# A third place for Q's and K's halves in the head of an attention-plus-MLP kernel, with two buffers of rows to be turned in place of three

## The chip, the core and the metric

The kernel runs on one core of a Trainium2 chip. TensorE (PE) multiplies matrices into PSUM, ScalarE (ACT) and VectorE (DVE) work on tiles, GpSimd (POOL) does small things, and DMAs are issued from the queues of SyncE (SP), POOL and ACT. Each engine works through its own instructions in the order of the program; engines wait for one another by semaphores. The metric is the device time of one execution in microseconds. The time before is the median of three runs.

## What is computed

```python
x  = A_x                                   # 1 x 2048 x 640
xn = layernorm(x)
q, k, v = split(xn @ wqkv, 32 heads of 20)
p  = softmax(q @ k.T * 20 ** -0.5)         # per head, 2048 x 2048
a  = (p @ v) @ wo
y  = layernorm(xn)
m  = gelu(y @ w1 + b1) @ w2 + b2           # 640 -> 1536 -> 640
return x + a + m
```

## The kernel before

All matrix products of the projections and the MLP are made from pairs of 16-bit halves: a value is written as a high half and a low half in float16 (the low half is what the high half's rounding left), and a product is three matmuls (high by high, high by low, low by high; `PASS`, line 326).

The work has two stages. In the **head** (lines 175 to 665) x is normalised, turned so that features lie on partitions, and projected to Q, K and V, while the weights of the MLP are loaded, squared for their scale and split into halves. In the **main part** (from line 668) attention and MLP are woven together by hand on TensorE. Both stages have `tc.manual_schedule()`: what stands in the program first goes first on its engine, and nothing is reordered.

The head goes over four blocks of 512 tokens, `for c in range(4)` (line 585). For each block:

- `qk(c, tt)` for `tt` = 0 to 4 (lines 328 to 341, called at 593 and 598): 30 matmuls fill one PSUM tile with 256 features of Q or K for the 512 tokens.
- Then some slices of the weights' work, `some(n)` (line 534), or a step of the next block's norm: `norm_a`, `norm_b`, `norm_c` (lines 245 to 286). `norm_c` writes the reciprocal deviations to `rscr` in DRAM by a DMA that POOL issues (line 286).
- Then `qk_out(c, tt, ps)` (line 346): ScalarE writes the high half of the PSUM tile to `qkhl` (line 352), VectorE the low half (353), the squares of the high half are taken (`qk_sq`, 363), and two DMAs on SP's queue bring both halves to `qkscr` in DRAM (358). The tile `qkhl` is of the pool `st`, tag `ks`, which has two buffers; a buffer is free again once its two DMAs have landed and its squares are taken. Later the same two buffers take the attention's K tiles.
- In the blocks c = 1 and c = 2, behind the outputs tt = 2, 3 and 4, `turn(nxt, j)` (line 312, called at 627 to 629) prepares the next block: j = 0 behind tt = 2, j = 1 and 2 behind tt = 3, j = 3 behind tt = 4. ScalarE writes the high half of 128 tokens' rows to `row` (318), VectorE the low half (319), and a transposing DMA on SP's queue turns it into the block's tile `xnt` (320). A buffer of `row` is free again when its transpose has landed. Behind j = 3 the whole turned block is written to `xscr` (323). Block 1 is turned on TensorE instead (`transp`).
- Then four `vproj(c, j)` (line 404): 30 matmuls each, for V of 128 tokens, with their output `vproj_out` (416).

All these PSUM tiles, and the small ones for scales (`mxp`, line 112), go round in the three buffers of tag `s` of the pool `psS`: a matmul that takes a buffer waits until the tile of three allocations before has been read. `pow2` (line 104) sums a tile of squares over partitions by a matmul with ones (line 114); `factors()` (456) does so for the bias `b1t`, whose square ScalarE takes through `squares` (97). In block c = 1 `factors()` and the first slice of w2's split (139 to 141) are the slices called at tt = 4, between the product `qk(1, 4)` and its output.

`junk` is a scratch that receives the elementwise results of square activations whose only wanted output is the sum (`accum_out`). `sums("k", ...)` and `sums("v", ...)` (lines 605 and 611) take the squares of K's and V's weights.

After `load_x(3)` on SP's queue (line 633) block 3's rows come to the tiles `xt`; `norm_a(3)` reads them at c = 2, tt = 0.

Of the kernel before, what the change touches and what calls it, by code (L numbers as in the profile page):

```python
# [10 lines left out]
F16 = mybir.dt.float16  # L11
BF16 = mybir.dt.bfloat16
# [6 lines left out]
P = 128  # L19
S, D, H, DH, F = 2048, 640, 32, 20, 1536  # L20
KD = D // P
# [23 lines left out]
def mha_mlp_kernel(tc, x, wqkv, wo, w1, b1, w2, b2, out):  # L45
# [4 lines left out]
    with (  # L50
# [40 lines left out]
        def squares(ws, junk):  # L91

            acc = sm.tile([P, 8], F32, tag="acc", name="acc")
            for i, w in enumerate(ws):
                j = junk[:, : w.free_size()] if len(w.shape) == 2 else (
                    junk[:, : w.shape[1] * w.shape[2]].rearrange("p (a b) -> p a b", a=w.shape[1]))
                nc.scalar.activation(j, w, AF.Square, accum_out=acc[:, i : i + 1])
            return acc[:, : len(ws)]
# [76 lines left out]
        with tc.tile_pool(name="pa", bufs=2) as pa, tc.tile_pool(name="pa1", bufs=1) as pa1, tc.manual_schedule():  # L175
            wv = pa1.tile([P, KD, 3, 2, D], F16, name="wv")

            stage = {}
# [96 lines left out]
            def norm_b2(c):  # L275
                mv, ve, r, r2 = rs[c]

                nc.vector.tensor_mul(ve, r, r)
                nc.vector.scalar_tensor_tensor(ve, ve, 2.0**-20, mv[:, :, 1], ALU.mult, ALU.mult)
                nc.vector.tensor_scalar(ve, ve, EPS, None, ALU.add)  # L280
                nc.gpsimd.tensor_tensor(r2, ve, nhalf, ALU.pow)

            def norm_c(c):
                mv, ve, r, r2 = rs.pop(c)
                newton(r2, ve, "b")
                nc.gpsimd.dma_start(rscr[c * 512 : (c + 1) * 512].rearrange("(j p) -> p j", p=P), r2)
# [25 lines left out]
            def turn(c, j):  # L312

                if j == 0:
                    xnts[c] = pa.tile([P, KD, 2, 512], F16, tag="xnt", name=f"xnt{c}")
                xv = xts[c][j].rearrange("p (k n) -> p k n", k=KD)
                row = pa.tile([P, KD, 2, P], F16, tag="row", name="row", bufs=3)
                nc.scalar.activation(row[:, :, 0, :], xv, AF.Copy)
                nc.vector.tensor_sub(row[:, :, 1, :], xv, row[:, :, 0, :])
                nc.sync.dma_start(xnts[c].rearrange("p k s t -> p (k s) t")[:, :, j * P : (j + 1) * P],  # L320
                                  row.rearrange("p k s n -> p (k s n)"), transpose=True)
                if j == 3:
                    nc.sync.dma_start(xscr[:, :, :, c * 512 : (c + 1) * 512], xnts[c])
                    del xts[c]
# [16 lines left out]
                return ps  # L341

            norms = [None, None]
            pend = []

            def qk_out(c, tt, ps):
                hl = stp.tile([P, 2, 2, 512], F16, tag="ks", name="qkhl")

                parts = ((0, 2),) if tt != 2 else ((0, 1), (1, 2))
                for i0, i1 in parts:  # L350
                    a = qks[:, (2 * tt + i0) // KD : (2 * tt + i0) // KD + 1]
                    nc.scalar.activation(hl[:, 0, i0:i1], ps[:, i0:i1], AF.Copy, scale=a)  # L352
                    nc.vector.scalar_tensor_tensor(hl[:, 1, i0:i1], ps[:, i0:i1], a, hl[:, 0, i0:i1],  # L353
                                                   ALU.mult, ALU.subtract)
                if c + tt > 0:
                    qk_sq(c, tt, hl)
                for s in range(2):
                    nc.sync.dma_start(
                        qkscr[s, 2 * tt * P : (2 * tt + 2) * P, c * 512 : (c + 1) * 512]
                        .rearrange("(i p) t -> p i t", p=P), hl[:, s])  # L360
                return hl

            def qk_sq(c, tt, hl):
                if tt % 2:
                    sq = stp.tile([P, S // 2], F16, tag="qs", name="sq").bitcast(BF16).rearrange("p (i t) -> p i t", i=2)
                else:
                    sq = pa.tile([P, 2, 512], BF16, tag="sq", name="sq", bufs=2)
                if c == 0:
                    nc.scalar.activation(sq, hl[:, 0], AF.Square)
                else:  # L370
                    nc.vector.tensor_mul(sq, hl[:, 0], hl[:, 0])
                pend.extend((c, 2 * tt + i, sq[:, i]) for i in range(2))
# [50 lines left out]
                                                   ALU.mult, ALU.subtract)  # L423

            qks = pa1.tile([P, 2], F32, name="qks")
            junk = pa1.tile([P, 3 * D], BF16, name="junk")
            accs = {}

            def sums(tag, ws):
                accs[tag] = squares(ws, junk)  # L430
# [97 lines left out]
            def ask(n):  # L528
                for _ in range(n):
                    next(asked, None)  # L530
# [3 lines left out]
            def some(n):  # L534
                for _ in range(n):
                    next(slices, None)
# [48 lines left out]
            for c in range(4):  # L585
                nxt = c + 1 if c < 3 else None
                for tt in range(5):
                    if c == 0 and tt == 1:
                        norm_b2(0)
                        norm_c(0)  # L590

                        nc.scalar.activation(junk[:, :1], ones[:, :1], AF.Exp)
                        ps = qk(0, 1, lambda: scale_of("k"))
                        hl = qk_out(0, 0, first)
                        split_qkv("q", c0=4 * P)
                        split_qkv("k")
                    else:
                        ps = qk(c, tt)
                    if tt == 3:
                        lengths(4)  # L600

                    if c == 0:
                        if tt == 0:
                            split_qkv("q", c0=2 * P, c1=4 * P)
                            sums("k", [stage["k"][:, 0:3], stage["k"][:, 3:]])
                            first = ps
                            continue
                        elif tt == 1:
                            qk_sq(0, 0, hl)
                        elif tt == 2:  # L610
                            sums("v", [stage["v"][:, 0:3], stage["v"][:, 3:]])
                            norm_a(1)
                        elif tt == 3:
                            scale_of("v")
                            split_qkv("v")
                    else:

                        step = tt - (c == 1)
                        if nxt and 0 <= step < 3:
                            (norm_a, norm_b, norm_c)[step](nxt)  # L620
                            some(1)
                        else:
                            some(2)
                    qk_out(c, tt, ps)

                    ask((0, 1, 2, 2, 1)[tt] if c == 0 else 0)
                    if nxt and c > 0 and tt >= 2:
                        for j in ((0,), (1, 2), (3,))[tt - 2]:
                            turn(nxt, j)
                    if c == 3 and tt == 2:  # L630
                        early = [load_features(mc) for mc in range(2)]
                if c == 1:
                    load_x(3)
                if c == 3:
                    stack = load_stack(0, 0)
                    for _ in range(6):
                        next(stack)
                for j in range(4):
                    ps = vproj(c, j)
                    if j == (0 if c == 3 else 1):  # L640
                        lengths(10)
                    if c + j > 0:

                        vproj_out(c, j, ps)
                    if c == 0:
                        if j < 2:
                            (norm_b, norm_c)[j](1)

                        pts = []
                        for k in ((), (0,), (2, 4), ())[j]:  # L650
                            transp(1, k, pts)
                        for t in pts:
                            transp_out(*t)
                    if j == 0 and c == 3:
                        shifts()
                        for _ in stack:
                            pass
                    some(1 if c == 3 else 2 if j < 3 or c == 0 else 0)
                    if c + j == 0:
                        vproj_out(c, j, ps)  # L660
                    if c == 0:
                        ask(2 if j == 0 else 1)
                if c == 0:
                    load_x(2)
# [678 lines left out]
```

## Time and profile before

| | us |
|---|---|
| runs: median of 3 | 1332.87 |
| lowest and highest run | 1332.36, 1333.18 |
| the profiled execution: its span | 1337.9 |
| its distance from the median of the runs | 5.0 |
| TensorE busy | 1325.8 |
| ScalarE busy | 1128.0 |
| VectorE busy | 1055.1 |

For the profiled execution its span is the only time there is: from the first instruction to the last. A row of the timeline gives an instruction's (or some merged instructions') start and duration, the engine, the line of the kernel, the operation, output and inputs, shapes and count; in brackets how long the engine was idle before it, and what ended the wait. A row of the waits gives who waited for whom, the microseconds in total, how often, and the longest. A row of the windows gives, for a stretch, its length, the busy time of each engine with the count of its instructions, the clock that TensorE was granted, the DMA engines' share and GB/s. In rows of the timeline a queue is written SPq, and PEld is TensorE's weight load.

### The profile page before, as it was taken

What the parts mean: (1) busy time and instruction counts of PE and PEld (TensorE: products, weight loads), DVE (VectorE), ACT (ScalarE), POOL (GpSimd) and SP (SyncE); (2) the same over time, 40 slices, a digit from 0 to 9 for tenths busy, and PEclk for the clock granted to TensorE, in tenths of its full rate; (3) what the DMA queues carried; (4) which work ended last, traced back from release to release, by engine and by line L of the source; (5) the groups of instructions that cost most, each with busy time, mean ns of one, the idle gap of its engine ahead of it and who ended that gap; (6) DMA issues with size and microseconds to landing.
All of it is one profiled execution on the core that took longest, in us unless ns stands there. A gap on an engine that the chain in (4) does not pass through costs nothing.

```text
span 1337.9 us, 29042 instructions
## 1 busy us (share of the span) xinstructions
PE 1325.8 (99%) x11635; PEld 586.7 (44%) x11635; DVE 1055.1 (79%) x1431; ACT 1128.0 (84%) x1306; POOL 37.5 (3%) x86
## 2 busy tenths in 40 slices
PE   9999899999999999999999999999999999999998
PEld 6645456444434343434343443344443434333366
DVE  7656754998788989878897879888879888997742
ACT  7844334999999999999999999999999999999900
POOL 3010000000000000000000000000000000000000
PEclk9999899999999999999999999999999999999999
DMA  9778723021203232212322132223032323334375
GB/s 279 254 196 176 136 79 104 15 59 39 66 28 103 61 83 81 63 48 59 111 63 81 33 93 66 75 69 94 19 80 71 93 66 87 118 95 118 105 218 188
DMA packets 100326, 129.54 MB, mean 97 GB/s; under 512 B 24292, under 2 KB 66664, under 8 KB 100188
## 3 DMA queue, kind: packets, MB, share of 16 engines
q1 hardware_dynamic: 96652, 120.25, 31.6%
q0 software_dynamic: 2912, 6.90, 2.8%
q8 instruction: 92, 1.51, 0.5%
q10 hardware_dynamic: 624, 0.51, 0.1%
q14 instruction: 46, 0.38, 0.1%
HBM read 82.14 MB, written 42.51 MB: 93 GB/s over the span
## 4 chain that ended last, share of the span: by engine, by line
PE 87%; DVE 6%; DMA 4%; ACT 1%; issue 1%; SPq 0%; ACTq 0%; DVEq 0%
PE o L779 30%; PE s L748 20%; PE py L1061 13%; PE pu L1031 11%; PE z L1146 5%; PE qkp L337 5%; PE vp L410 3%; DVE low L762 2%; DMA xt<-in_A_x_dram 1%; DMA xnt<-row 1%; DMA qkscr<-qkhl 1%; DVE st L255 1%; DVE qkhl L353 1%; ACT p L750 1%; DMA wos<-in_A_wo_dram 0%
## 5 line engine op out<-in xcount | busy, mean ns | idle before, releaser
L750 ACT ACTIVATE p<-s 128x1024 f32<-128x1024 f32 x1024 | 973.9, 1050 | 33.1 <-PE s L748 27.1
L762 DVE TENSOR_TENSOR low<-p 128x1024 f16<-128x1024 f32 x512 | 614.3, 1218 | 144.8 <-ACT p L750 144.0
L779 PE MATMUL o<-p,vfull 128*32 128x512 bf16 (+1 forms) x4096 | 429.0, 493 | 0.0
L748 PE MATMUL s<-qs,ks 61*128 61x512 f16 x2048 | 311.4, 381 | 0.2 <-ACT p L750 0.2
L748 PEld LDWEIGHTS <-ks 61*128 61x128 f16 x2048 | 61.2, 94 | 278.4 <-issue 276.1
L1061 PE MATMUL py<-w2t,hT 128*128 128x320 f16 x1152 | 178.5, 300 | 0.0
L1031 PE MATMUL pu<-xm,w1t 128*128 128x256 f16 x1440 | 178.2, 273 | 0.1
L1031 PEld LDWEIGHTS <-w1t 128*128 128x128 f16 x1440 | 131.0, 98 | 64.0 <-issue 50.2
L1061 PEld LDWEIGHTS <-hT 128*128 128x128 f16 x1152 | 102.3, 98 | 88.1 <-issue 53.9
L337 PE MATMUL qkp<-xnt,wv 128*128 128x512 f16 x600 | 131.1, 379 | 1.3 <-issue 1.3
L779 PEld LDWEIGHTS <-vfull 128*32 128x32 f16 x3072 | 59.9, 95 | 138.4 <-issue 106.9
L779 PE MATMUL o<-low,vfull 128*32 128x512 f16 x1024 | 101.3, 377 | 0.1
L337 PEld LDWEIGHTS <-wv 128*128 128x128 f16 x600 | 58.2, 98 | 71.0 <-issue 1.6
L779 PEld LDWEIGHTS o<-p,vfull 128*32 128x32 f32 x2048 | 61.7, 108 | 53.2
L410 PE MATMUL vp<-wv,xnt 128*128 128x320 f16 x480 | 69.5, 306 | 3.7 <-DVE qkhl L353 3.7
L1146 PE MATMUL z<-w1t,ot 128*128 128x320 f16 x480 | 67.4, 299 | 0.0
L352 ACT ACTIVATE qkhl<-qkp,qks 128x1024 f16<-128x1024 f32 (+1 forms) x24 | 23.1, 964 | 46.3 <-PE qkp L337 26.6
L410 PEld LDWEIGHTS <-xnt 128*128 128x128 f16 x480 | 47.9, 100 | 23.8 <-issue 3.7
L1146 PEld LDWEIGHTS <-ot 128*128 128x128 f16 x480 | 46.0, 98 | 22.9 <-issue 5.5
L353 DVE SCALAR_TENSOR_TENSOR qkhl<-qkp,qks,qkhl 128x1024 f16<-128x1024 f32 (+1 forms) x24 | 26.5, 1104 | 32.9 <-ACT qkhl L352 32.9
L1103 DVE SCALAR_TENSOR_TENSOR acc<-z,sc,acc 128x320 f32<-128x320 f32 x32 | 17.5, 549 | 37.3 <-PE z L1146 37.2
L800 ACT ACTIVATE ev<-o 128x512 f32<-128x512 f32 x64 | 39.5, 618 | 2.2 <-PE o L779 2.1
(195 smaller groups left out, 670.4 us busy)
## 6 DMA issues: line engine op xcount, KB each, us to landing
qkscr<-qkhl SPq DMA_DIRECT2D x40, 256.0 KB
opart<-ev SPq DMA_DIRECT2D x124, 80.0 KB
ks<-qkscr SPq DMA_DIRECT2D x120, 80.0 KB
qs<-qkscr SPq DMA_DIRECT2D x192, 40.0 KB
oa<-opart SPq DMA_DIRECT2D x32, 240.0 KB
xt<-in_A_x_dram SPq DMA_DIRECT2D x16, 320.0 KB
xscr<-xnt SPq DMA_DIRECT2D x4, 1280.0 KB
xm<-xscr SPq DMA_DIRECT2D x8, 640.0 KB
```

The costliest lines, as they stand in the source:

```text
L337: nc.tensor.matmul(ps[:, i, :], wv[:, k, q, a, mm * P : (mm + 1) * P], xnts[c][:, k, b, :], start=(k + n == 0), stop=(k == KD - 1 and n == 2))
L352: nc.scalar.activation(hl[:, 0, i0:i1], ps[:, i0:i1], AF.Copy, scale=a)
L353: nc.vector.scalar_tensor_tensor(hl[:, 1, i0:i1], ps[:, i0:i1], a, hl[:, 0, i0:i1], ALU.mult, ALU.subtract)
L410: nc.tensor.matmul(ps[:, hf, :320], xnts[c][:, k, a, j * P : (j + 1) * P], wv[:, k, 2, b, hf * 320 : (hf + 1) * 320], start=(n == 0), stop ...
L748: nc.tensor.matmul(ps[:, a, :], ks[64 * a : 64 * a + 61, kb * P : (kb + 1) * P], qs[64 * a : 64 * a + 61, cc * 512 : (cc + 1) * 512], star ...
L750: nc.scalar.activation(pt, ps, AF.Exp, scale=QS)
L762: nc.vector.tensor_sub(low, pt, upper(pt))
L779: nc.tensor.matmul(pv.o[32 * q : 32 * q + 32, :], src[:, v0 - PAD * (1 - q % 2) :][:, :32], t, start=q not in pv.begun, stop=last, skip_gr ...
L800: nc.scalar.activation(evs[g, hf][:, cc], pv.o, AF.Copy)
L1031: nc.tensor.matmul(ps[:, i], w1v[:, k, (f + i) // 4, a, fo_ : fo_ + P], xnt[:, k, b, :], start=(n == 0), stop=(n == 3 * KD - 1))
L1061: nc.tensor.matmul(ps[:, :320], hTs[mc][:, f, a, j * P : (j + 1) * P], w2v[:, f, b, hf * 320 : (hf + 1) * 320], start=(n == 0), stop=(n == ...
L1146: nc.tensor.matmul(ps[:, :320], ot[:, k, a, j * P : (j + 1) * P], wov[:, k, b, h * 320 : (h + 1) * 320], start=(n == 0), stop=(n == 3 * KD ...
```

## The change

Three edits, all in the head.

1. The tile of rows to be turned (`row`) has two buffers, the pool's default, in place of three.
2. `qk_out` counts its calls. Each third tile `qkhl` gets a place of its own (pool `pa1`, one buffer, tag `hl`); the others go round in the two buffers of tag `ks` as before. So there are three places in turn.
3. `junk` is 1536 elements long in place of 1920, and the squares of K's and V's weights (five slabs of 640) are taken in three pieces (2, 2 and 1 slabs) in place of two (3 and 2).

```diff
@@ turn
-                row = pa.tile([P, KD, 2, P], F16, tag="row", name="row", bufs=3)
+                row = pa.tile([P, KD, 2, P], F16, tag="row", name="row")
                 nc.scalar.activation(row[:, :, 0, :], xv, AF.Copy)
                 nc.vector.tensor_sub(row[:, :, 1, :], xv, row[:, :, 0, :])
@@ qk_out
             norms = [None, None]
+            outs = [0]
             pend = []
 
             def qk_out(c, tt, ps):
-                hl = stp.tile([P, 2, 2, 512], F16, tag="ks", name="qkhl")
+                outs[0] += 1
+                third = outs[0] % 3 == 0
+                hl = (pa1 if third else stp).tile([P, 2, 2, 512], F16, tag="hl" if third else "ks", name="qkhl")
@@ scratch
-            junk = pa1.tile([P, 3 * D], BF16, name="junk")
+            junk = pa1.tile([P, F], BF16, name="junk")
@@ the head's loop
-                            sums("k", [stage["k"][:, 0:3], stage["k"][:, 3:]])
+                            sums("k", [stage["k"][:, 0:2], stage["k"][:, 2:4], stage["k"][:, 4]])
...
-                            sums("v", [stage["v"][:, 0:3], stage["v"][:, 3:]])
+                            sums("v", [stage["v"][:, 0:2], stage["v"][:, 2:4], stage["v"][:, 4]])
```

## The prediction

> **What bounds the kernel now.** First the page: its span and its busy row.
>
> ```profile
> span 1337.9 us, 29042 instructions
> PE 1325.8 (99%) x11635; PEld 586.7 (44%) x11635; DVE 1055.1 (79%) x1431; ACT 1128.0 (84%) x1306; POOL 37.5 (3%) x86
> ```
>
> TensorE is busy for 1325.8 of 1337.9 us. All that the diff touches runs in the head, before the attention's first score matmul at 224.70 in the timeline. Second, TensorE's waits up to 226 us, and then ScalarE's (line waited for: us in total, times, longest).
>
> ```profile
> PE vp L410 <- DVE qkhl L353: 3.7, 1, 3.7
> PE qkp L337 <- issue: 1.3, 1, 1.3
> ...
> ACT row L318 <- DMA xnt<-row: 6.5, 1, 6.5
> ACT qkhl L352 <- DMA qkscr<-qkhl: 6.3, 1, 6.3
> ```
>
> TensorE loses only 3.7 + 1.3 us to waits in the whole head. ScalarE waits 6.3 us for a place of Q's and K's halves (qkhl), which a third place can take away, and 6.5 us for a buffer of rows (row), of which there will be one less. So I look for where these two waits sit. The timeline around the turning of block 2's rows (c = 1; start, duration, engine, line):
>
> ```profile
> 94.36 1.35 ACT L318 ACTIVATE row<-xt 128x640 f16<-128x640 f32 x2
> 94.47 1.49 SPq L320 DMA_TRANSPOSE xnt<-row  x1
> 94.74 0.79 POOL L286 DMA_DIRECT2D rscr<-r  x1 [3.21 <-DVE lo L117]
> 95.61 0.20 ACT L97 ACTIVATE junk<-b1t 128x12 bf16<-128x12 f32 x1
> 95.71 0.19 ACT L97 ACTIVATION_READ_ACCUMULATOR junk<-b1t 128x1 f32 x1
> 95.80 0.82 ACT L139 ACTIVATE wtmp<-w2t,s 128x640 f32<-128x640 f32 x1
> 100.24 0.28 PE L114 MATMUL mxp<-acc,ones 128*128 128x1 f32 x2
> 100.38 8.31 PE L410 MATMUL vp<-wv,xnt 128*128 128x320 f16 x60
> 100.49 1.11 ACT L352 ACTIVATE qkhl<-qkp,qks 128x1024 f16<-128x1024 f32 x1 [3.87 <-issue]
> 103.64 1.27 DVE L353 SCALAR_TENSOR_TENSOR qkhl<-qkp,qks,qkhl 128x1024 f16<-128x1024 f32 x1
> 108.14 0.74 ACT L318 ACTIVATE row<-xt 128x640 f16<-128x640 f32 x1 [6.54 <-DMA xnt<-row]
> 111.57 1.36 SPq L320 DMA_TRANSPOSE xnt<-row  x1
> 113.83 3.56 PE L410 MATMUL vp<-wv,xnt 128*128 128x320 f16 x25
> 118.66 26.06 PE L337 MATMUL qkp<-xnt,wv 128*128 128x512 f16 x120 [1.26 <-issue]
> 119.20 3.89 SPq L192 DMA_DIRECT2D xt<-in_A_x_dram  x4
> ```
>
> Rows 1 and 2 of the four (counted from 0) are written at 94.36 as a pair. Row 3 has to wait for row 0's buffer, that is for the landing of the transpose issued at 94.47, until 108.14. Nothing on TensorE needs that row soon, so the wait is free today but for the 1.26 us at 118.66, where Q and K of block 2 wait for the block's turned rows. The same stretch for block 3 (c = 2), and the clock around it:
>
> ```profile
> 125.88 0.88 DVE L255 BATCH_NORM_STATS2 st<-xt 128x6 f32<-128x320 f32 x2
> 140.19 0.77 POOL L286 DMA_DIRECT2D rscr<-r  x1 [2.00 <-DVE r L243]
> 144.72 1.38 SPq L320 DMA_TRANSPOSE xnt<-row  x1
> 144.99 6.65 PE L337 MATMUL qkp<-xnt,wv 128*128 128x512 f16 x30
> 151.63 1.11 ACT L352 ACTIVATE qkhl<-qkp,qks 128x1024 f16<-128x1024 f32 x1 [6.30 <-DMA qkscr<-qkhl]
> 152.64 1.35 ACT L318 ACTIVATE row<-xt 128x640 f16<-128x640 f32 x2
> 155.12 1.10 ACT L352 ACTIVATE qkhl<-qkp,qks 128x1024 f16<-128x1024 f32 x1
> 156.11 0.73 ACT L318 ACTIVATE row<-xt 128x640 f16<-128x640 f32 x1
> 158.17 1.28 DVE L353 SCALAR_TENSOR_TENSOR qkhl<-qkp,qks,qkhl 128x1024 f16<-128x1024 f32 x1
> 159.50 6.88 PE L410 MATMUL vp<-wv,xnt 128*128 128x320 f16 x30 [3.67 <-DVE qkhl L353]
> 159.96 0.82 DVE L319 TENSOR_TENSOR row<-xt,row 128x640 f16<-128x640 f32 x1
> ...
> 158.00:159.00 1.00, 0.00 (x0) 0.00 (x0) 1.00 (x2) 0.69 (x2) 0.00 (x0) 0.55 1.08 210
> 164.00:165.00 1.00, 1.00 (x5) 0.59 (x4) 0.73 (x2) 0.00 (x0) 0.00 (x0) 0.53 0.00 0
> ```
>
> The last two rows are of the windows view; the number after POOL's pair is the granted clock. Here the 6.30 us wait for a qkhl place makes the next output late: ScalarE at 155.12, VectorE at 158.17 to 159.45. That frees the PSUM place which the second block of V needs, and TensorE stands for 3.67 us. The clock falls to a half at about 158.1 and is back at about 164.9, so TensorE works 5.4 us, from 159.50 on, at half speed: another 2.7 us. This place costs 3.67 + 2.7 = 6.4 us, and it is what the third place can win back.
>
> **The change, part by part.**
>
> *Two buffers of rows.* Row 2 now takes row 0's buffer, so the wait moves from row 3 forward to row 2, in ScalarE's order from 108.14 up to the second of the pair at 94.36. That second one started at about 94.36 + 1.35 - 0.74 = 95.0. What stands behind it on ScalarE is no longer harmless: the square of b1t (95.61), its accumulator (to 95.90), a weight split (95.80), and the output of the last Q/K product (100.49). The b1t sum feeds the two small mxp matmuls, and these stand on TensorE at 100.24, ahead of all of V's product (100.38). TensorE works in order, so it will stand from 100.24 until row 2, b1t and the sum are done. With row 2 at 108.14, the sum is ready 95.90 - 95.0 = 0.9 us later, at 109.05, and V's product starts some 0.35 us after that, near 109.4 instead of 100.38: 9.0 us lost.
>
> Does the landing stay at 108.14? It isn't governed by how many transposes queue up, but by the 2 KB write of rscr in four-byte pieces, issued by POOL right behind the transpose:
>
> ```profile
> rscr<-r POOLq DMA_DIRECT2D x4, 2.0 KB, 11.6
> ```
>
> (page, DMA issues; the last number is the median to landing.) 94.74 + 11.6 = 106.3, and the transpose is seen 1.8 us later. Neither issue moves. Bounds: not before 106.3 if rscr holds it (1.8 us less), not after 108.14 + 1; I take 108.14. The Trainium skill ("DMA: Bandwidth & Descriptors", Queues, rings and completion order) says that a DMA's semaphore increment lands only after every earlier write of that DMA engine, across its queues. By that rule the landing cannot come before rscr's writes are through; the 108.14 agrees.
>
> The clock: a gap of 3.67 us was enough to halve it, so one of 9 us is. The nearest row says 2.7 us for the way back; with the 6.8 us of half clock used in full it would be 3.4, and with a restart late in them as little as 1.5. The Trainium skill ("TensorE: Matmul & The Clock Gate", The HAM clock gate) counts some 3.4 us at half speed after a restart, which would be 1.7 us; the trace has 5.4 us at half speed, and the measurement goes into the sum.
>
> The output behind (ScalarE near 110, VectorE near 113.8 instead of 103.64, done by 115.1) frees the PSUM place for V's second block, due at 109.4 + 4.1 + up to 2.7, about 116: just in time. V's four blocks took 100.38 to 117.39, so they end near 109.4 + 17.0 + 2.7 = 129.1. The last row's transpose is issued near 116.5 (VectorE's part stands behind the late output; 111.57 before), so it lands before 129 and the 1.26 us at 118.66 is gone. Q and K of block 3 start at 129.1 instead of 118.66: **+10.4 us**.
>
> *The third place.* The fourth output of c = 2 takes the place of the first, not the second, whose transfer was late; the 6.30 us wait goes. What is late next: row 2 again, now waiting for the transpose of 144.72. With 108.14 - 94.74 = 13.4 us after rscr's issue it lands at about 140.19 + 13.4 = 153.6 in the old frame (estimate; the row at 156.11, which had no wait, bounds it from above). With nothing else changed ScalarE would then reach the next output at about 155.4 instead of 155.12, VectorE, with one row's subtraction (0.82) already done, at 157.2 instead of 158.17, and TensorE would still stand 2.7 us.
>
> But VectorE has a lead now. Its long queue in c = 2 starts with the statistics at 125.88, when the x rows land (issued at 119.20 on SP, behind the last transpose). That transpose moves by 116.5 - 111.57 = 5 us, TensorE by 10.4. So VectorE's chain, up to the rscr write of 140.19, comes about 5 us earlier in TensorE's time, and so does the landing: 148.6. Row 2 then ends at 149.3 and the split behind it near 150.6, before the last Q/K product ends at 144.99 + 6.65 = 151.64. The output goes at 151.7, VectorE is through by 154.2, and V's second block, due at 155.8, doesn't wait. **-3.67 - 2.7 us.** Bounds for this part: -6.4 to -1.0.
>
> *Squares of K's and V's weights in three pieces, shorter scratch.* The same elements, one more activation and accumulator each:
>
> ```profile
> 20.84 1.79 ACT L97 ACTIVATE junk<-w2t 128x1920 bf16<-128x1920 f32 x1
> 22.75 1.27 ACT L97 ACTIVATE junk<-w2t 128x1280 bf16<-128x1280 f32 x1
> 25.15 0.28 PE L114 MATMUL mxp<-acc,ones 128*128 128x2 f32 x2
> 25.29 15.70 PE L337 MATMUL qkp<-xnt,wv 128*128 128x512 f16 x72
> ```
>
> A piece of 1920 takes 22.75 - 20.84 = 1.91 us with its accumulator, one of 1280 about 1.4, one of 640 about 0.86 (by the slope), so three take 3.65 against 3.3: 0.35 us more. K's sum, done near 24.1, is due at 25.15, so that is hidden; the K weights' split behind it feeds TensorE closely. Bounds 0 and 0.4 us; I take 0.2. For V's sum VectorE's statistics are the later wait: nothing.
>
> *The sum:* 9.0 + 2.7 - 1.3 - 3.7 - 2.7 + 0.2 = +4.2 us on the profile's span of 1337.9. The profiled execution is 5.0 us longer than the median of the runs (1332.87); I carry the difference over: **1337.1**. The rest of the program is fed by TensorE's own pace and only moves.
>
> **The rivals.**
>
> *The first transpose lands in time (faster).* If, with less in SP's queue, row 0's transpose landed before 100.24 - 0.9 = 99.3, row 2 would wait on nobody's account and only the 6.4 us would be won: about 1326.7. The time falls one for one with the landing; it decides at about 108.14 - 4.2 = 103.9. For it: the bare issue takes 1.49 us. Against it: rscr's 11.6 us. By the ordering rule quoted above it can't happen while rscr is issued there. 0.08; landings between some 103 and 106.5, no measurable difference, 0.14.
>
> *The second stall stays.* If VectorE has no lead, only 1.0 of the 6.4 us is won: +9.6, 1342.5. For it: x rows and wo's pieces arrive by DMA, not at TensorE's pace. Against it: only 1 to 2 us of the 5 are needed. 0.15. By the Trainium skill ("TensorE: Matmul & The Clock Gate", The HAM clock gate) the clock falls after an idle window of some 3.4 us, so that a stand of 2.7 us would cost no clock and this case would give 1339.8; the trace's clock fell 2.3 us into the idle time, so I don't count on it.
>
> *The freed wait is no place at all:* were the 6.30 us owed to SP's queue and not to the place, the third place would give nothing, and the result is that of the case before it. In its 0.15.
>
> **How the numbers follow.** The forecast, 1334.5 to 1339, has 0.58; slower for a cause I don't see (tiles of the attention lying on other old ones) 0.05. About 0.2% (2.7 us) is what a measurement of this kernel can tell from no change: 1330.2 and 1335.5 are the borders. Below the first: 0.08. Between: 0.14 and about 0.08 of the forecast's lower end, 0.22. Above: 0.70. The range, 1332 to 1342.5, leaves out the fast rival, the earliest landings and half of the slow case: under 0.2.
>
> **What would show it.** TensorE's largest wait in the head at its mxp matmul near 100, some 9 us, released by ScalarE's b1t; ScalarE's wait for the transpose of row 0 at the second row of the pair; the clock at a half behind it; no idle time before Q and K of block 3; no wait of ScalarE on qkscr<-qkhl, and none of V's product on L353. It is wrong if that ScalarE wait is under 9 us, or if V's product still stands in block 3.

## The result and the profile after

| | median, us | lowest to highest | runs |
|---|---|---|---|
| before | 1333.06 | 1332.36 to 1334.49 | 5 |
| changed | 1341.60 | 1341.00 to 1344.01 | 5 |

The ratio is 1.0066 (1.0054 to 1.0079): 8.5 us slower. The forecast was +4.2 us, 1337.1. The profiled execution of the changed kernel tells something else at first sight: its span is 1338.9 us, only 1.0 us over the 1337.9 of before. The same execution took 1341.0 us by the clock that the runs are timed with, so 2.1 us lie outside the span. By that difference the profile of before belongs to an execution of about 1340.0 us (an estimate), though the five runs shown of before end at 1334.5. That will be the point on which the sum failed.

The changed kernel, the waits of TensorE and of ScalarE up to 226 us (line waited for: us in total, times, longest; from line 346 on its lines are numbered three higher than before):

```profile
PE mxp L114 <- ACT junk L97: 6.5, 1, 6.5
PE warm L235 <- POOL ones L197: 1.1, 1, 1.1
...
ACT row L318 <- DMA xnt<-row: 18.0, 3, 10.9
```

Before, TensorE stood for 3.7 us ahead of V's second block of c = 2 and for 1.3 us ahead of the Q/K product of block 2; both waits are gone. In their place stands the b1t sum, for 6.5 us, behind ScalarE's square (L97). ScalarE now waits 18.0 us for transposes of rows, 6.5 before, and no longer for places of qkhl. The timeline of the changed kernel around the turning of block 2's rows:

```profile
94.16 1.49 SPq L320 DMA_TRANSPOSE xnt<-row  x1
94.43 0.79 POOL L286 DMA_DIRECT2D rscr<-r  x1 [3.18 <-DVE r L243]
94.80 0.73 ACT L318 ACTIVATE row<-xt 128x640 f16<-128x640 f32 x1
106.40 0.74 ACT L318 ACTIVATE row<-xt 128x640 f16<-128x640 f32 x1 [10.87 <-DMA xnt<-row]
107.04 0.20 ACT L97 ACTIVATE junk<-b1t 128x12 bf16<-128x12 f32 x1
107.38 0.58 PE L114 MATMUL mxp<-acc,ones 128*128 128x1 f32 x2 [6.48 <-ACT junk L97]
107.83 9.73 PE L413 MATMUL vp<-wv,xnt 128*128 128x320 f16 x60
```

Row 1 is written at 94.80, row 2 only at 106.40, when row 0's transpose, issued at 94.16, has landed. b1t's square, which before stood at 95.61, follows at 107.04, and TensorE takes the sum at 107.38. The 60 matmuls of V behind it take 9.73 us; before they took 8.31. The windows of the same kernel (after the pair of POOL: granted clock, DMA share, GB/s) show why V is slower:

```profile
104.00:106.00 2.00, 0.00 (x0) 0.00 (x0) 0.00 (x0) 0.00 (x0) 0.00 (x0) 0.50 1.33 76
108.00:110.00 2.00, 2.00 (x9) 1.14 (x8) 1.69 (x15) 1.05 (x2) 0.00 (x0) 0.50 1.15 237
110.00:112.00 2.00, 2.00 (x14) 1.31 (x13) 1.90 (x8) 0.00 (x0) 0.00 (x0) 0.81 1.16 88
```

All engines stand from 104 to 106, and the clock is at a half by then. A mean of 0.81 over 110 to 112 means half speed until about 110.8. In c = 2, where block 3's rows are turned, the changed kernel goes on without a stop:

```profile
145.81 0.77 POOL L286 DMA_DIRECT2D rscr<-r  x1 [2.00 <-DVE r L243]
150.34 1.38 SPq L320 DMA_TRANSPOSE xnt<-row  x1
152.20 1.11 ACT L355 ACTIVATE qkhl<-qkp,qks 128x1024 f16<-128x1024 f32 x1 [1.27 <-PE qkp L337]
158.05 0.74 ACT L318 ACTIVATE row<-xt 128x640 f16<-128x640 f32 x1 [4.11 <-DMA xnt<-row]
159.92 1.09 ACT L355 ACTIVATE qkhl<-qkp,qks 128x1024 f16<-128x1024 f32 x1
161.69 1.28 DVE L356 SCALAR_TENSOR_TENSOR qkhl<-qkp,qks,qkhl 128x1024 f16<-128x1024 f32 x1
163.13 4.24 PE L413 MATMUL vp<-wv,xnt 128*128 128x320 f16 x30
```

The fourth output of c = 2 goes at 152.20, as soon as its product is there; row 2 waits 4.11 us for its buffer, the next output follows at 159.92, VectorE is through at 162.97, and V's second block starts at 163.13 with no idle time: by a hair. The landing keeps its distance from the write of rscr, not from the transpose's own issue: row 2 is written 7.7 us after the transpose was issued (150.34) and 12.2 us after the write (145.81); in block 2 it was 12.2 and 12.0 us.

### The profile page after: what moved, and what is told of

It reads as the page before. It is cut to its first block, busy times and chain, and to the rows that moved or that the text cites. A ratio compares the mean times of both kernels' runs of the same rounds, so it can differ in the third digit from the quotient of the medians.

```text
span 1338.9 us, 29043 instructions
## 1 busy us (share of the span) xinstructions
PE 1325.0 (99%) x11635; PEld 586.4 (44%) x11635; DVE 1055.4 (79%) x1431; ACT 1129.5 (84%) x1310; POOL 37.5 (3%) x86
## 4 chain that ended last, share of the span: by engine, by line
PE 90%; DVE 5%; DMA 2%; ACT 1%; issue 1%; SPq 0%; DVEq 0%; ACTq 0%
PE o L782 29%; PE s L751 19%; PE py L1064 12%; PE pu L1034 11%; PE qkp L337 8%; PE vp L413 5%; PE z L1149 5%; DVE low L765 2%; DMA xnt<-row 1%; ACT p L753 1%; DMA w1t<-in_A_wqkv_dram 0%; DMA oscr<-oa 0%; ACT junk L97 0%; DVE hT L984 0%; DVE u L971 0%
## 5 line engine op out<-in xcount | busy, mean ns | idle before, releaser
L356 DVE SCALAR_TENSOR_TENSOR qkhl<-qkp,qks,qkhl 128x1024 f16<-128x1024 f32 (+1 forms) x24 | 26.5, 1105 | 28.1 <-ACT qkhl L355 28.1
```

## The experiments

Each run is compared with runs of the kernel before on the same chip. Theory A: in a usual run the kernel before has little to win back, so the wait for the first transpose is the whole cost. Theory B: V's stand of 3.7 us and the half clock are usual, and the third place wins them back. Where the first transpose's lateness comes from, and why it costs what it does, is asked along with it.

**The kernel before once more (b0_again).** No edit.

> The kernel before, unchanged, profiled once more. The profiled execution shown of it has a span of 1337.9 us, while the changed kernel's one has 1338.9 us in a run of 1341.0: 2.1 us lie outside the span. So a usual run of 1332.9 should have a span of about 1330.8, 7 us under the profile that the prediction was worked from. Theory A (that profile was an uncommon execution): this profile has a span near 1331, TensorE does not stand before V's second block of c = 2, and the clock is not halved near 158. Theory B (the stand is usual, and the profile is longer all over): a span near 1338, with the 3.7 us stand again. Ratio 1.000 under both.

12 runs, 1332.34 to 1338.54 us, median 1335.28; the kernel before beside it 1332.05 to 1339.38 in 29 runs. Its profile, the span and the waits of TensorE and of ScalarE:

```profile
span 1333.6 us, 29042 instructions
...
PE vp L410 <- DVE qkhl L353: 0.4, 1, 0.4
...
ACT qkhl L352 <- DMA qkscr<-qkhl: 4.5, 2, 3.1
```

V stands for 0.4 us in place of 3.7, and the clock isn't halved there (1.00 from 156 to 162). The span is neither the 1331 of theory A nor the 1338 of theory B. Most of what it has above 1331 comes from another place: in this execution the clock is at a half from 11.7 to 15.1 us, and the first Q/K product starts at 16.79, where it started at 14.69 in the first profile of before.

```profile
12.00:14.00 2.00, 2.00 (x11) 2.00 (x11) 0.81 (x2) 1.06 (x4) 0.00 (x0) 0.50 1.09 367
```

So the kernel before varies by itself, and not in one place only. Over the three chips used here, 29 of its 82 runs took more than 1335.8 us, up to 1341.75. Every run over 1339.2 had a mean granted clock of 0.997 or less; those under 1332.7 had 0.999 or 1.0. Half speed for the 6.8 us of the first profile lowers the mean of a run by 0.0026, so the short runs hold no such stretch. The profile behind the prediction was one of the long ones. The five runs beside the result held none. This is theory A, for the runs of the result.

**Two buffers of rows alone (rows2, rows2_again).**

```diff
-row = pa.tile([P, KD, 2, P], F16, tag="row", name="row", bufs=3)
+row = pa.tile([P, KD, 2, P], F16, tag="row", name="row")
```

> Two buffers of rows alone. Theory A (usual runs before have nothing to win back, so the change's whole cost is the wait for the first transpose and the half clock behind it): +8 us, ratio 1.006, TensorE standing some 6.5 us at the b1t sum near 100 us. Theory B (the third place wins back 6.4 us that this kernel doesn't get): slower than the full change by about 6 us, +15 us, ratio 1.011.

1.0058 (1.0041 to 1.0075), median 1342.64. Its waits of TensorE:

```profile
PE mxp L114 <- ACT junk L97: 7.3, 1, 7.3
PE vp L410 <- DVE qkhl L353: 1.5, 1, 1.5
```

The whole slowdown is there without the third place (and without the squares in three pieces). A second time, side by side with the changed kernel:

> Two buffers of rows with two places. Theory A (the third place wins nothing here, since row 2 waits on ScalarE for the same write as the place did): within 1 us of the changed kernel. Theory B (the third place is worth V's stand of 1.5 us and sometimes the clock): 1.5 to 4 us slower than the changed kernel.

> The changed kernel once more, on the same chip and beside the same runs of before as the next two. Stand of 6 to 9 us at the b1t sum, ratio 1.003 to 1.007, lower the more runs of before fall in its slower group (1336 to 1342 us, V's stand with the half clock).

Changed kernel 1341.54 us, 1.0049 (1.0033 to 1.0064); two buffers alone 1341.51, 1.0044 (1.0029 to 1.0059). Here 9 of the 23 runs of before were over 1335.8, which lowers both ratios against the result; the medians of the changed kernel are 0.06 us apart on the two chips. The wait of TensorE at the b1t sum, and ScalarE's for a place of qkhl, in rows2_again:

```profile
PE mxp L114 <- ACT junk L97: 5.9, 1, 5.9
...
ACT qkhl L352 <- DMA qkscr<-qkhl: 0.3, 1, 0.3
```

This profile has no stand of V in c = 2 at all, though it has two places. With two buffers, the third place is worth nothing that shows; the two kernels also differ by the squares, which cost 0.3 us.

**The same change with row 2 behind the last output (late2).**

```diff
-for j in ((0,), (1, 2), (3,))[tt - 2]:
+for j in ((0,), (1,), (2, 3))[tt - 2]:
```

> The full change, but row 2 is written behind the last Q/K output (tt = 4) with row 3, so that b1t's square and that output no longer stand behind the wait for the first transpose. If that order is the cause, the 6.5 us stand and the half clock go: within 2 us of before (ratio 0.999 to 1.002), with at most 1 to 2 us at the start of block 2's Q and K, which wait for the last transpose. If the cost comes from the new places in memory or from the DMAs, it stays at 1.006.

1.0001 (0.9991 to 1.0011), median 1334.35, all 12 runs between 1333.33 and 1335.53. The b1t sum doesn't wait any more; V's stand of 1.5 us in c = 2 is the only one left behind 90 us. So what costs is what stands behind row 2 on ScalarE, not memory or the buffer as such. The same order without the third place:

> Two buffers of rows, two places, and row 2 written behind the last output (tt = 4) as in late2. It differs from late2 only by the third place and the squares. If the third place is what keeps V's stand short in block 3, this one shows runs of 1336 to 1340 us beside late2's 1333.3 to 1335.5 and a stand of over 2 us; if the order of the rows does it, it is as late2: 1333 to 1336, ratio near 1.000.

1.0013 (0.9999 to 1.0026), median 1336.94, 1335.50 to 1338.42. The one row that differs in the waits of TensorE, first of this kernel:

```profile
PE vp L410 <- DVE qkhl L353: 2.6, 1, 2.6
```

and then of late2:

```profile
PE vp L413 <- DVE qkhl L356: 1.5, 1, 1.5
```

V's stand is 1.1 us shorter with the third place, ScalarE doesn't wait for a place (3.8 us without it), and the longer runs are missing. So here the third place seems to do what it is for. But the two intervals overlap and the runs are of two chips, so some 1 to 2 us is a reading, not a measurement. The third place with three buffers of rows, and rscr where it was, has not been run.

**The write of rscr behind the turning (rscr_late).** The changed kernel, with POOL's 2 KB DMA for the blocks 2 and 3 held back until the third V block (j = 2):

```diff
                 newton(r2, ve, "b")
+                if c > 1:
+                    held.append((c, r2))
+                else:
+                    write_r2(c, r2)
+
+            held = []
+
+            def write_r2(c, r2):
                 nc.gpsimd.dma_start(rscr[c * 512 : (c + 1) * 512].rearrange("(j p) -> p j", p=P), r2)
...
                     some(1 if c == 3 else 2 if j < 3 or c == 0 else 0)
+                    if j == 2 and held:
+                        write_r2(*held.pop())
```

> The full change, but the 2 KB write of rscr for the blocks 2 and 3 is issued behind the third V block, after the turning. If the first transpose's landing is held up by that write, it lands some 3 to 5 us after its issue, near 98 us; row 2 then waits 2 to 4 us, the b1t sum is ready before 100 us and TensorE doesn't stand: ratio 0.997 to 1.002. If a first transpose takes its 10 us by itself or by what SP's queue holds, TensorE stands 4 to 7 us as before and the ratio stays at 1.004 to 1.007.

0.9997 (0.9986 to 1.0007), median 1333.52. Its timeline, against the one shown above of the changed kernel, and behind it its wait of TensorE in c = 2:

```profile
93.92 1.49 SPq L328 DMA_TRANSPOSE xnt<-row  x1
97.59 0.74 ACT L326 ACTIVATE row<-xt 128x640 f16<-128x640 f32 x1 [2.19 <-DMA xnt<-row]
100.60 0.28 PE L114 MATMUL mxp<-acc,ones 128*128 128x1 f32 x2
...
138.36 0.77 POOL L294 DMA_DIRECT2D rscr<-r  x1 [2.00 <-DVE r L243]
...
PE vp L421 <- DVE qkhl L364: 0.7, 1, 0.7
```

The transpose, issued at 93.92, has landed by 97.59: 3.7 us, where it took 12.2 (94.16 to 106.40) with the write beside it. Row 2 waits 2.19 us, and TensorE doesn't stand. The row at 138.36 is a flaw of this edit: for block 3 nothing ahead of it kept POOL, which issued the write as early as ever, so only block 2 was freed, and V still stands for 0.7 us. It serves as a control within the same run: block 3's transpose, issued at 142.89, lands only by 150.49, which is 12.1 us after that write.

**b1t's square earlier (b1_early).** The changed kernel with `squares([b1t], junk)` called at c = 1, tt = 2, ahead of the rows.

> The full change, but b1t's square is taken one output earlier, ahead of the rows that wait, so that the b1t sum at 100 us no longer waits. If only that sum were the cause, the stand goes and the ratio falls to 1.000. By my theory the last Q/K output is still behind row 2 on ScalarE, so TensorE runs V's first block and then stands before the second until VectorE has ended that output, some 4 to 6 us, with the half clock: ratio 1.003 to 1.006.

1.0054 (1.0035 to 1.0073), median 1345.11. Its waits of TensorE:

```profile
PE vp L413 <- DVE lo_b L115: 5.7, 1, 5.7
PE vp L413 <- DVE qkhl L356: 3.8, 1, 3.8
```

and V's second block in c = 2:

```profile
166.25 7.12 PE L413 MATMUL vp<-wv,xnt 128*128 128x320 f16 x30 [3.77 <-DVE qkhl L356]
```

The stand at the b1t sum has only moved. V's first block runs, and the second waits 5.7 us. My expectation named the wrong last link: it isn't the output of Q/K but VectorE's reading of the b1t sum (lo_b), whose PSUM place V needs; that reading is queued behind row 2's low half, so behind the same transpose. And in c = 2 V stands 3.8 us here, with the third place, because row 2 waits there too; the clock falls again (30 matmuls of V in 7.12 us, 4.24 in the changed kernel). So the third place is no safeguard.

**TensorE kept busy in the gap (kept_busy).** The changed kernel with 26 matmuls of ones ahead of the b1t sum; their result is not used.

> The full change, with 26 more matmuls of ones (their output is not used) ahead of the b1t sum on TensorE, so that it is busy for 5 to 6 of the 6.5 us for which it would stand. They delay nothing that isn't late already, and keep the clock up. If the half clock behind the stand costs 1.4 us or more, as in the changed kernel's trace (60 matmuls of V in 9.73 us for 8.31), the kernel is 1 to 3 us faster than the full change: ratio 1.004 to 1.006. If the clock costs nothing, it stays at 1.0066.

1.0046 (1.0029 to 1.0064), median 1342.84, beside runs of before of which 13 of 30 were over 1335.8. In its profile row 2's buffer came later than in the changed kernel (107.83), TensorE still stood for 2.4 us, and the clock fell to a half all the same, from about 109.2 to 112.6, 0.3 us after the stand had ended:

```profile
PE mxp L116 <- ACT junk L97: 2.4, 1, 2.4
```

Its twelve runs do have a higher mean clock, 0.997 to 1.0, than the fourteen of the changed kernel (0.995 to 0.997), and they are no shorter (1342.84 against 1341.60 and 1341.54, on other chips). A gain of 1 to 3 us from the clock does not show. With the later landing beside it, the clock's price can't be read from this run either way.

**The whole step norm_c behind the third V block (b_norm_late, a_norm_late).** With this the write meets no turning in either block; once on the kernel before, once on the changed one.

```diff
-(norm_a, norm_b, norm_c)[step](nxt)
+(norm_a, norm_b, lambda c: None)[step](nxt)
...
+if j == 2 and 0 < c < 3:
+    norm_c(c + 1)
```

> The kernel before, with three buffers of rows and two places, but the step that ends in the 2 KB write of rscr (norm_c) is called behind the third V block for the blocks 2 and 3, so that the write no longer meets a turning. If that write is what makes the transposes and the transfers of Q's and K's halves late in both blocks, ScalarE's waits for them (6.5 and up to 6.3 us) and V's stand of 0.4 to 3.7 us go, and with them the runs of 1336 to 1339: 1330 to 1332.5, ratio 0.997 to 0.9995, with a narrower spread. If not, 1.000 and the same spread.

> The changed kernel with the same edit (norm_c behind the third V block for the blocks 2 and 3). With the write out of the way two buffers of rows should do: no stand at the b1t sum, and the time within 1 us of the kernel before with the same edit, ratio 0.997 to 1.000. If two buffers cost something by themselves, it stays above 1.002.

Before with this edit: 1332.55 us, 0.9966 (0.9950 to 0.9982), 10 of 12 runs under 1333.6. Changed kernel with it: 1332.19 us, 0.9966 (0.9948 to 0.9984), all 10 runs under 1333.9. Neither has a wait of TensorE over 1.1 us in the head. First the kernel before with it, ScalarE's only wait for a place of qkhl:

```profile
ACT qkhl L352 <- DMA qkscr<-qkhl: 0.3, 1, 0.3
```

then the changed kernel with it, ScalarE's waits for rows:

```profile
ACT row L318 <- DMA xnt<-row: 7.0, 3, 3.7
```

The kernel before is faster with the edit than without it on the same chip. The changed kernel was not run there without it, but took 1341.6 and 1341.5 us on two other chips. With the edit both are alike. With the write out of the way two buffers of rows do as well as three, and two places as well as three; both cuts together were not run. As the chip of these two had many long runs of before, the ratio holds their removal; against the shortest run of before there (1332.37) the shortest of these are 0.2 and 0.8 us faster.

## Why the prediction was right in sign and short in size

1341.6 us lies above the forecast's 1334.5 to 1339 and near the upper end of the range, 1342.5, which was set by another case. That it fell inside is in part luck.

*Two buffers of rows: right, with 9.0 us where 6.5 were measured.* Row 2 waits for row 0's transpose and the b1t sum waits for row 2, as said. The landing came at the lower bound (106.40, 12.0 us after rscr's issue), not at 108.14 (13.4 us). Other executions had stands of 5.9, 6.2 and 7.3 us.

*That rscr's write holds the transpose up: right, and now shown.* Without it the transpose lands 3.7 us after its issue. In every profile in which a row waits for that transpose beside the write, the row starts 11.6 to 13.8 us after the write's issue. How the write does it is open. The Trainium skill ("DMA: Bandwidth & Descriptors", Queues, rings and completion order) says that a DMA's semaphore increment lands only after every earlier write of that DMA engine, across its queues. The prediction drew from it that the landing can't come before rscr's writes; but rscr is issued 0.27 us behind the transpose in block 2, and no run shows whether its writes count as earlier. Nor do the runs tell that rule from slow memory writes that hold up all DMA traffic alike.

*The clock: right, 2.7 us taken, 1.4 measured* in V's 60 matmuls (9.73 against 8.31), because only the last 3.4 of the 6.8 us at half speed fell behind the restart; the prediction had 1.5 for that. In the second profile of the changed kernel (after_again) the half speed lasted 10.2 us, and the same matmuls took 2.7 us more:

```profile
107.55 11.02 PE L413 MATMUL vp<-wv,xnt 128*128 128x320 f16 x60
```

*The 1.26 us before block 2's Q and K: gone*, as said.

*The third place, -6.4 us: this is the step that failed.* In the profile of the changed kernel V's stand and the half clock are gone, and the two profiled executions differ by +1.0 us: 6.5 + 1.4 - 1.3 - 6.4 + 0.3 (the squares) = 0.5, and some 0.3 us of the b1t sum itself at half clock. But the sentence "I carry the difference over" to the median of the runs was wrong. The profile of before was of a long execution, and the second profile of before has 0.4 us to win there, not 6.4. The 5.0 us between span and median, noted and left unexplained, was the warning: a span should be about 2 us shorter than a run, not 5 us longer. With 0.4 in place of the 6.4 and no wait ahead of block 2's Q and K, as in that second profile, the sum is 6.5 + 1.4 to 2.7 + 0.3 + 0.3 - 0.4 = 8.1 to 9.4 us, an estimate made after the fact, against 8.5 measured. The case that gave 1342.5 (V's stand stays) came nearest in time for another reason: there was hardly a stand to lose. That it was the third place which took the stand away in the changed kernel isn't shown either: rows2_again has none with two places, and b1_early has 3.8 us with three.

*VectorE's lead: smaller than said.* The statistics of the next block's rows (norm_a at c = 2) start 5.6 us later than before (131.48, 125.88), the Q and K of c = 2 7.4 us later (126.10, 118.66): a lead of 1.8 us, not 5. V's stand was gone in this profile and in that of rows2_again, and not in those of rows2 (1.5 us) and b1_early (3.8). What decides between them is open. The bounds of -6.4 to -1.0 were meant for a stand of 3.7 us, which the runs of the result hardly had.

*Squares in three pieces: 0.2 us taken, 0.3 measured.* From the first Q/K matmul to the first norms (lines 382 and 385) it is 26.23 us before (14.69 to 40.92) and 26.53 after (14.89 to 41.42). The other profiles agree to 0.02 us: 26.2 with two pieces, 26.5 with three.

*Two slips that change nothing.* TensorE's 3.7 + 1.3 us are not all its waits in the head: another 1.9 us (1.1, 0.6 and 0.2) lie in the first 15 us, which the change doesn't touch. And the Q and K that start at 118.66 are block 2's, which the prediction calls block 3's where it sums up the first part.

## What to carry to other kernels

Before a saving is read from one profile, hold its span against the runs: if it is longer than what they leave for it, the stall in it may belong to that execution and not to the kernel. A buffer less doesn't only add a wait; it moves the wait forward in its engine's order. What counts is which small instruction, here a square of 0.2 us, is queued behind it, and who needs that at once. When several waits end together, look for the one slow transfer that they share: moving one 2 KB write did more than a place or a buffer.

## What the runs showed of the hardware

- A DMA of 2 KB in four-byte pieces takes 9.2 to 12.6 us to land (the median of its four in each of the thirteen profiles). A transpose issued beside it takes 12.2 us to land (the changed kernel, block 2), where it takes 3.7 without it (rscr_late).
- In eight stands behind 90 us the clock fell to a half: for 6.8 us in six of them, for 10.2 in after_again and for 3.4 in kept_busy. The fall came 2.0 to 5.1 us after TensorE had stopped; in kept_busy 2.7 us after 6 us of matmuls of ones, when V had just begun. Stands of 0.4, 0.7, 1.5 and 2.6 us behind 90 us (b0_again, rscr_late, late2, rows2_late2) left it up.
- A long stand is not needed: in b0_again and a_norm_late the clock also fell to a half for 3.4 us, from 11.7 and 11.1 us on, with no stand of over 1.0 us in the 8 us before.
- Identical runs of the kernel before differ by up to 9.4 us on one chip (1332.37 to 1341.75).
